# Retention followed by a GELU MLP on one core: the first w_in half triggered one step earlier, the second w_in part loaded in two halves, and a new table of the order

## The chip, the cores and the metric

The kernel runs on one core of a Trainium2 chip. The metric is the device time of one execution in microseconds, the median of 3 runs. Engines: PE is TensorE (matmuls; PEld its weight loads), DVE is VectorE, ACT is ScalarE, POOL is GpSimd, SP is SyncE. SP and ACT issue transfers on two hardware queues (q1 and q10 in the profile), POOL on a software queue (q0).

## The reference, cut to what matters

```python
# q, k, v: (4, 8, 768, 64)     w_in: (512, 2048)     w_out: (2048, 512)
state = zeros(4, 8, 64, 64); gamma = 1 - 2.0 ** (-5 - arange(8))
for t in range(768):
    state = gamma * state + outer(k[:, :, t], v[:, :, t])
    y[:, :, t] = 0.125 * q[:, :, t] @ state
x = y.transpose(0, 2, 1, 3).reshape(4 * 768, 512)
out = gelu_tanh(x @ w_in) @ w_out          # (3072, 512), float32
```

## The kernel before, in words

The recurrence is done in 6 chunks (c = 0 to 5) of 128 time steps, each for the 4 batches (b). For a chunk and a batch, q and k are scaled and cast to 16 bits (line 239; in `prep1` and `cast_in`), transposed on PE (T: line 274 in chunk 0, line 285 later) and evicted (`qkT`, line 222 on ACT, line 224 on DVE), multiplied with each other (A: line 296), masked by DVE (line 347), multiplied with v (Y: line 327) and evicted as x (line 222 on ACT). The state update is S (line 338), the part from the old state is line 315.

The MLP's first product M1 takes chunk 0 plainly (`m1_first`, matmuls in `moe1_mm`, line 428): 8 pairs of output blocks, fp = 0 to 7, each as a wide group (8 matmuls of 256 columns: batches 0 and 1) and two narrow ones (8 matmuls of 128 columns: batch 2, batch 3). The other chunks go by a scheme with 7 products instead of 8 on sums of blocks (line 551 for M1, lines 574 and 563 for M2). DVE and POOL make the sums (line 453), ACT the GELU (line 444).

w_in comes in 4 parts of 512 columns (`load_w_in`, line 409), w_out in 4 parts (`load_w_out`, line 418), all triggered by POOL and cast from 32 to 16 bits on the way. The first part of w_in is loaded in two halves (lines 601 and 602). In POOL's queue they stand behind the casts of k for batches 0 and 1 and ahead of the one for batch 2. The pair fp = 0 needs the first half alone, fp = 1 the second half (line 969: the tokens `winh` and `win`).

Before line 621 the instructions stand in the order in which the code writes them. From there on, `op` and `pe` make numbered items with needs and gives, and the table ORDER (lines 16 to 71) says in which sequence they are issued: a letter for the engine (p = PE, v = DVE, a = ACT, g = POOL, s = SP) and the item's number. "w1" is one filler matmul of line 190. The items of kind "trig" are the other 7 triggers of weights; "hold" (line 782) is a small copy on POOL that waits for the third part of w_out, and all later loads by SP (line 793) wait for it. Constants such as LANDS (line 772) and the lines 1164 and 1192 are landing times that the planner of the table assumed; they are not in the program that runs.

At the end, the last chunk's output is stored in pieces (lines 1147 to 1159): two 256 KB stores by ACT, one of 256 KB and two of 128 KB by SP. Each needs the evictions of its part.

Of the kernel before, what the change touches and what calls it, by code (L numbers as in the profile page):

```python
# [13 lines left out]


ORDER = """
p169 v9 v10 a168 a8 g0 g1 g2 g3 p181 g4 g5 g6 p179 w1 p174 a173 p172 v170 a180 p191 a190
p177 v171 g11 g7 s12 s13 p185 a178 v176 s14 s15 s16 g26 v175 s17 g29 s18 s19 s20 s21 v140
s22 g32 s23 v160 v161 g35 v163 v144 v145 v136 v141 v148 v149 p183 a182 v150 v137 v156 v157
p193 a192 p189 p187 p207 a186 p209 a208 v158 v152 v153 p223 a206 p225 p227 v138 a224 p229  # L20
v155 p195 a194 p197 a222 a228 p211 p213 a196 p231 p233 a226 a212 a210 v146 p199 p201 p215
p203 a198 a214 a202 a200 p846 v147 p217 a216 p219 p221 a218 v164 v24 a184 p847 p235 a230
a232 v25 a188 a234 p205 a204 p848 p849 v139 a220 p850 p851 p852 v165 p853 p237 v162 s36 s37
v27 v28 p240 s38 s39 s40 a238 a239 p854 p855 a856 p243 v242 v241 p246 a245 a244 p858 a859
v154 p861 g49 p249 p262 p265 p864 p865 a264 v30 v247 v248 v142 p267 v31 a236 a862 s41 p252
v166 v33 v34 a266 a250 s42 a251 s43 s44 s45 v143 s46 p866 p331 a332 p258 v151 a256 p255 p333
p316 v257 p261 v253 v254 p314 a315 v260 v259 v334 g50 v317 p867 a868 p263 p269 v268 p271
a270 p275 v274 a318 g276 g278 p297 p280 a298 a281 g55 g277 g56 s47 s48 s863 s857 g279 p299
v300 p282 v283 a335 a301 g52 g53 p273 p304 v272 a305 p287 a288 g58 g59 s61 s62 s63 s869 p338
g51 s64 p285 p302 v167 a339 a286 p292 a303 a284 g54 p309 v293 a294 s65 v310 a311 p289 p306  # L30
p378 v290 a291 v376 v377 v307 p336 a337 p343 v344 p295 a296 p319 a320 v348 p321 a322 p366
v364 p372 v365 a371 v370 a308 p323 v324 p312 a313 g352 p369 v367 p384 a382 a383 p326 v327
a328 g353 g57 a345 p340 v341 a342 v368 p329 a330 p375 v373 g60 p381 v380 v374 p870 p346 a347
g360 g361 g354 v379 p871 a325 s66 a872 p387 v385 v386 p388 p389 p391 s860 v390 p395 p393
v392 p399 v394 p401 p397 v396 g402 g404 p873 p442 s67 v400 p440 a441 p406 a407 p874 v443
v875 g349 g403 a444 p408 v409 p413 p423 p425 a414 a424 p411 v398 v426 v356 g357 v159 p457
a412 a410 p428 p418 v419 a458 a429 p430 a431 v359 g70 a78 p415 a72 a82 p459 v460 a461 p432
p447 p435 v436 g74 a76 a427 s68 s69 s86 v416 a80 a448 a437 p876 p877 p445 a446 p879 p880
g362 g405 g350 g84 s87 p464 a465 a420 p452 p462 p421 v363 g77 v79 a878 p449 a463 v83 v433
a422 g81 v355 v358 p438 a434 a417 v450 v453 p469 v470 p882 p455 p883 g476 a881 p466 a451  # L40
v351 a454 v474 v71 a439 v75 s88 a456 p885 g482 v478 g483 v467 p501 v499 p492 a500 v490 v491
g73 g85 p886 v887 a468 g475 s888 a471 p472 a473 v884 g480 s89 g95 s90 s91 s92 p893 p495 v493
g479 g486 p507 g97 v506 p504 v503 v502 v494 p889 p890 a891 s892 p894 g487 s93 p498 p509 p508
v505 p515 p511 v496 v497 p517 p521 p519 a103 a895 p513 v510 v512 a99 v514 a107 v96 p896 p897
p543 a544 v516 g522 p562 g524 p526 a527 p560 v520 v898 g105 g523 g101 g485 g102 s94 s111
a561 v518 v484 p899 p545 p900 s112 s113 g477 g525 g98 a901 p528 v529 v104 a530 p550 p548
a551 a549 s114 g110 v563 v546 a547 a564 v489 p565 p531 p902 g481 p555 p533 v556 a534 a532
v488 p567 p903 p538 a557 a109 a566 a568 v539 a540 p535 g106 v536 a537 v100 p552 v553 p905
p577 p541 a904 p906 a554 a542 a578 p584 p558 p569 p572 v108 v907 p582 v570 v573 a571 v596
a559 v594 v598 v595 s115 v599 a585 p579 v580 p908 p909 v910 s911 a583 g601 a574 s116 p575  # L50
a120 a576 g602 g603 p589 g600 g122 p586 v587 v590 p612 a581 a591 v611 p621 a588 a610 v620
p912 p913 p592 a593 v606 v607 p916 p917 a914 a619 g604 p618 s117 s118 p615 v613 v614 p624
g123 v623 a918 v617 s119 p919 p920 p922 v921 p923 g608 s915 a924 v622 p627 v616 p629 p628
p631 v625 v626 p633 v630 p639 p635 v634 v632 v638 p641 v597 p637 v636 g609 a132 g124 p925
p926 p680 p663 a664 a927 g128 g642 g644 v129 g643 p665 v666 p646 v605 a647 p648 v649 a650
v640 v133 a681 g645 p928 p929 p682 p653 v683 a654 p931 p697 a698 a126 p651 a652 p668 a669
a667 p932 v131 v933 p658 v659 g135 a684 p704 a660 p655 p670 v656 a705 v930 a671 p672 p702
v121 a703 v673 a657 p685 p661 a662 p675 p687 a688 v714 v676 v715 a674 g127 p706 s934 v707
a686 p678 a677 a679 g130 g134 g718 g719 p699 v700 p935 a701 p709 v710 a708 p689 a711 v690
a691 p936 a937 s938 p692 v693 a694 p939 p695 p712 a696 a713 v722 g716 p741 v740 v724 p732  # L60
a730 a739 p940 a941 p942 p943 v726 v727 v723 p945 p946 g725 g720 g729 v717 p747 a731 p735
v125 p738 a947 v728 v944 g721 v746 v733 v734 v736 p948 p949 a950 v745 p951 p952 v737 p748
v953 p744 p749 v742 p954 v743 p751 p753 v750 v752 p757 v756 p755 v754 g758 p955 v956 s957
g760 p796 a797 p762 a763 p779 a780 p764 v765 g759 p798 p813 v799 p815 p786 a814 v816 a800
p781 a766 v782 a787 p784 a785 p818 a819 p767 a768 p801 p788 a817 p791 v792 a783 v789 g761
p769 a770 p820 a821 p771 v772 p822 p774 p803 p777 v775 v823 a790 a793 a802 p794 a804 a795
a776 v834 g835 a773 a824 a778 p825 v826 a827 p805 v806 p808 v809 a810 g832 p962 p958 v836
p811 p828 a829 v842 a812 v830 v831 a807 v838 v843 v839 g841 a963 p959 a960 s961 p964 p966
p968 g844 g837 v840 p970 a965 p972 v845 v833 v969 v967 a971 a973 p974 a975 p976 a977 p978
v979 p980 p983 v984 v981 s982 a985 p986 p989 v987 s988 p992 a990 a991 a993 s994  # L70
"""


# [1 line left out]
def kernel(  # L75
# [25 lines left out]
    g128 = gam ** 128.0  # L101
# [480 lines left out]
    def store(eng, o, p, c, a0, a1, n0=0, n1=512):  # L582
# [14 lines left out]
    o_evT(0, AC)  # L597
    load1(AC, "k", 0, 3)
    prep1(VE, "q", 0, 1)
    prep1(PO, "k", 0, 1)  # L600
    load_w_in(0, 0, 2)
    load_w_in(0, 2, 4)
    prep1(PO, "k", 0, 2)
    spin(3)
# [28 lines left out]
        trig="g",  # L633
# [135 lines left out]
            free=[ldk],  # L769
        )  # L770

    LANDS = [0, 19.8, 22.3, 25.4, 27.5, 30.1, 32.6, 35.1]

    def trig(nm, i, n):
        load = load_w_in if nm == "win" else load_w_out
        op("trig", lambda eng: load(i), [("trig", n - 1)], [(nm, i)], early=[("trig", n)], cost=LANDS[n])

    def hold():
        T["lq", "q", 1, 0] = tile_of("lq", 0)
# [169 lines left out]
    def m1_first():  # L949
        for t0, t1, bs, cost, kind in ((0, half, (0, 1), 0.873, "gelu"), (half, half + C, (2,), 0.45, "gelu2"),  # L950
                                       (half + C, 2 * half, (3,), 0.45, "gelu2")):
            for fp in range(NP):
                key = ("bank", "h", 0, fp, t0)

                def emit(fp=fp, t0=t0, t1=t1, key=key):
                    for r in range(2):
                        moe1_mm(0, 2 * fp + r, T[key][:, r, 0:t1 - t0], t0, t1)

                def ev(eng, fp=fp, t0=t0, t1=t1, key=key):
                    g_sb[0, fp // 2] = T["g", 0, fp // 2]  # L960
                    gelu(g_tile(0, 2 * fp)[:, :, t0:t1], T[key][:, :, 0:t1 - t0])

                new = fp % 2 == 0 and t0 == 0
                al = ("al", "g", 0, fp // 2)
                op(kind, ev, [key] + ([] if new else [al]), [("H0", fp, b) for b in bs],
                   alloc=[(("g", 0, fp // 2), 1)] if new else [], early=[al] if new else [],
                   free=[key])
                last = [("m1done", 0)] if fp == NP - 1 and t1 == 2 * half else []
                pe(cost, emit, [("x", 0, b) for b in bs] + [("win" if fp else "winh", fp // 2)] + after("M1", t0),
                   [key, ("m1part", 0, fp, t0)] + last,  # L970
                   [(key, 1, (128, 2, half))], [("x", 0)])

# [188 lines left out]

    for i in range(4):
        if i < 2:
            tok["winh" if i else "win", 0] = (16.6, 15.2)[i]
    tok["m1done", -1] = 0.0
    tok["al", "x", 0] = 0.0
    T["x", 0] = xT[0]
# [16 lines left out]
    for b in (2, 3):  # L1184
        for i, nm in enumerate("qkv"):
# [3 lines left out]
            held_by[key] = [p, n, 1, 0.0]  # L1189
            slots[p][n] = None  # L1190
            T[key] = raw[nm, 0, b]
            tok[key] = ((10.0, 11.0, 11.5), (12.4, 13.3, 15.0))[b - 2][i]
    slots["bank"] = [10.8, 12.3, 11.8, 13.6] + [12.9] * 4

    tok["trig", 0] = 9.4
    for n in range(1, 8):
        trig("win" if n < 4 else "wout", n % 4, n)
    hold()
    for b in (2, 3):
        for nm in "v" if b == 2 else "qkv":  # L1200
# [93 lines left out]
```

## Time and profile before

| | |
|---|---|
| median of 3 runs | 195.65 us (195.27, 195.65, 196.06) |
| the profiled execution | 196.41 us; its span from the first to the last instruction is 194.7 us |
| granted TensorE clock | 1.000 |
| PE busy | 187.6 us, 96% |
| DVE, ACT, POOL busy | 152.0, 125.3 and 112.3 us |
| PE busy from 0 to 12 us, 12 to 19.8, 19.8 to 180 | 9.52 of 12.00, 6.24 of 7.80, 160.18 of 160.20 |
| triggers of w_in | first half 8.67 us, second half 9.6, second part 11.4 |
| landings of these | 15.37, 18.2, 20.2 us |
| last matmul group ends, last eviction ends | 191.62, 192.02 us |

The "landing" of a transfer is the time at which the instruction that waits for it may go on. Busy times of a PE group include the time in which the next group already starts; the distance between the starts of two groups is what a group costs.

### The profile page before, as it was taken

How to read it: one execution, taken by the hardware profiler on the slowest of the kernel's cores; microseconds unless marked ns; L12 is line 12 of the kernel's file. 1: busy time of each engine (PE TensorE's matmuls, PEld its weight loads, DVE VectorE, ACT ScalarE, POOL GpSimd, SP SyncE). 2: the span in 40 equal slices, each digit the busy share in tenths (PEclk: the TensorE clock that was granted, in tenths of full speed). 3: DMA queues.
4: the chain of work that ended last, by engine and by line, in shares of the span. 5: the costliest groups of instructions: out<-in, count | busy, mean ns of one | idle time of the engine just before them, and what ended most of it. 6: DMA issues, size and time to landing. Idle time of an engine off the chain costs nothing.

```text
span 194.7 us, 6611 instructions
## 1 busy us (share of the span) xinstructions
PE 187.6 (96%) x2777; PEld 152.7 (78%) x2777; DVE 152.0 (78%) x295; ACT 125.3 (64%) x244; POOL 112.3 (58%) x122
## 2 busy tenths in 40 slices
PE   7787999999999999999999999999999999999993
PEld 2455997445788788888898888888888888888882
DVE  4375029979999999989998989699878788867940
ACT  3466557065599938999357978715699820799511
POOL 2695000021389989995999984965953570814520
PEclk9999999999999999999999999999999999999999
DMA  6999999999999667998799879960020200200205
GB/s 146 288 266 204 207 206 197 220 244 216 233 224 269 145 93 141 281 203 127 142 288 258 136 123 207 259 183 0 3 108 0 111 3 3 109 0 5 108 0 215
DMA packets 96285, 30.05 MB, mean 154 GB/s; under 512 B 88320, under 2 KB 93184, under 8 KB 96256
## 3 DMA queue, kind: packets, MB, share of 16 engines
q1 hardware_dynamic: 84976, 23.35, 51.5%
q0 software_dynamic: 4752, 4.19, 13.4%
q10 hardware_dynamic: 6528, 2.10, 4.3%
q8 instruction: 21, 0.34, 0.7%
q14 instruction: 8, 0.07, 0.1%
HBM read 27.54 MB, written 6.29 MB: 174 GB/s over the span
## 4 chain that ended last, share of the span: by engine, by line
PE 89%; DMA 7%; POOL 1%; ACTq 1%; ACT 0%; issue 0%
PE ps L563 32%; PE ps L551 32%; PE ps L574 7%; PE ps L428 7%; DMA w_in<-in_moe_w_in_dram 4%; PE ps L296 3%; DMA st<-in_k_dram 3%; PE ps L327 3%; PE ps L285 2%; PE ps L315 1%; PE ps L338 1%; ACTq L162 1%; POOL qk L239 1%; POOL w_in L409 0%; ACT o L222 0%
## 5 line engine op out<-in xcount | busy, mean ns | idle before, releaser
L453 DVE TENSOR_TENSOR st<-ps,st 128x512 f32<-128x512 f32 x60 | 39.0, 679 | 5.9 <-PE ps L551 4.1
L222 ACT COPY st<-ps 128x512 f32<-128x512 f32 x60 | 32.5, 592 | 14.5 <-PE ps L551 14.3
L444 ACT ACTIVATE g<-st 128x512 f16<-128x512 f32 x60 | 36.0, 643 | 4.6 <-DVE st L453 4.5
L551 PEld LDWEIGHTS <-w_in 128*128 128x128 f16 x320 | 30.9, 98 | 4.1
L563 PEld LDWEIGHTS <-s_g 128*128 128x128 f16 x320 | 30.8, 98 | 4.0
L347 DVE TENSOR_TENSOR a<-ps,mask 128x512 f16<-128x512 f32 x44 | 27.5, 681 | 4.1 <-PE ps L296 4.0
L222 ACT COPY o<-ps 128x512 f32<-128x512 f32 (+1 forms) x28 | 14.6, 529 | 21.0 <-PE ps L563 19.8
L444 ACT ACTIVATE g<-ps 128x512 f16<-128x512 f32 (+1 forms) x44 | 21.6, 528 | 7.5 <-PE ps L428 7.0
L453 POOL TENSOR_TENSOR s_g<-g 128x512 f16<-128x512 f16 x18 | 21.3, 1184 | 8.1 <-ACT g L444 6.6
L551 PEld LDWEIGHTS <-u_w 128*128 128x128 f16 x240 | 23.2, 98 | 2.8
L563 PEld LDWEIGHTS <-g 128*128 128x128 f16 x240 | 22.9, 98 | 3.1
L551 PE MATMUL ps<-xs,w_in 128*128 128x256 f16 x160 | 22.1, 273 | 0.0
L551 PE MATMUL ps<-xs,u_w 128*128 128x256 f16 x160 | 21.6, 273 | 0.0
L551 PE MATMUL ps<-x,w_in 128*128 128x256 f16 x160 | 20.8, 273 | 0.0
L563 PE MATMUL ps<-w_out,s_g 128*128 128x256 f16 x160 | 19.8, 273 | 0.0
L563 PE MATMUL ps<-w_out,g 128*128 128x256 f16 x160 | 19.6, 273 | 0.0
L563 PE MATMUL ps<-t_w,s_g 128*128 128x256 f16 x160 | 19.3, 273 | 0.0
L453 POOL TENSOR_TENSOR xs<-x 128x512 f16<-128x512 f16 x10 | 11.7, 1174 | 11.3 <-DVE x L354 9.7
L453 POOL TENSOR_TENSOR s_g<-g,s_g 128x512 f16<-128x512 f16 x10 | 11.9, 1199 | 9.0 <-DVE s_g L453 5.7
L453 POOL TENSOR_TENSOR s_g<-s_g,g 128x512 f16<-128x512 f16 x11 | 12.8, 1166 | 6.6 <-PE ps L551 5.9
L428 PE MATMUL ps<-x,w_in 128*128 128x128 f16 (+1 forms) x192 | 15.1, 237 | 1.3 <-DMA w_in<-in_moe_w_in_dram 1.3
L239 POOL TENSOR_TENSOR v<-ld,cst 128x512 f16<-128x512 f32 x15 | 16.3, 1105 | 0.0
(74 smaller groups left out, 292.3 us busy)
## 6 DMA issues: line engine op xcount, KB each, us to landing
ld<-in_v_dram SPq DMA_DIRECT2D x19, 256.0 KB, 4.5
ld<-in_k_dram SPq DMA_DIRECT2D x17, 256.0 KB, 4.2
out_dram<-o SPq DMA_DIRECT2D x8, 512.0 KB, 3.5
ldq<-in_q_dram SPq DMA_DIRECT2D x48, 64.0 KB, 2.7
w_out<-in_moe_w_out_dram POOLq DMA_DIRECT2D x4, 512.0 KB, 16.8
w_in<-in_moe_w_in_dram POOLq DMA_DIRECT2D x3, 512.0 KB, 10.4
ld<-in_q_dram SPq DMA_DIRECT2D x5, 256.0 KB, 5.0
out_dram<-o SPq DMA_DIRECT2D x5, 256.0 KB, 4.9
```

Source lines behind the costliest of these rows:

```text
L222: eng.copy(out=out, in_=in_)
L239: eng.tensor_tensor(out=o, in0=heads(src, sw), in1=heads(cst[:, col:col + H].unsqueeze(2), sw).broadcast_to([128, NHP, 2, Dh]), op=ALU.mult,)
L285: nc.tensor.transpose(out=ps[m][j * 64:(j + 1) * 64, n + i, hp], in_=h16[nm, c, b][rows, 2 * hp + j], identity=iden[rows, rows],)
L296: nc.tensor.matmul(out=ps[j][m * 64:(m + 1) * 64, hp], lhsT=t[j * 64:(j + 1) * 64, 1, hp, m * 64:(m + 1) * 64], rhs=t[j * 64:(j + 1) * 64, ...
L327: nc.tensor.matmul(out=ps[j * 64:(j + 1) * 64, hp], lhsT=h16["v", c, b][:, 2 * hp + j], rhs=a_sb[c, b, j][:, hp], start=(c == 0), stop=Tru ...
L347: eng.tensor_tensor(out=a_sb[c, b, j], in0=ps, in1=mask[:, j], op=ALU.mult)
L428: nc.tensor.matmul(out=out, lhsT=w_in_sb[wi][:, kc, wr * 128:(wr + 1) * 128], rhs=xT[c][:, kc, t0:t1], start=(kc == 0), stop=(kc == NHP - ...
L444: nc.scalar.activation(out=out, in_=in_, func=AF.Gelu_apprx_tanh, scale=1.0)
L453: eng.tensor_tensor(out=out, in0=in0, in1=in1, op=op)
L551: nc.tensor.matmul(out=ps[:, f], lhsT=m1_lhs(lk, kc, 2 * g + f), rhs=x[:, kc], start=(n in FIRST and kc == 0 and f == 0), stop=(n in (1, 5 ...
L563: nc.tensor.matmul(out=ps, lhsT=m2_lhs(c, lk, fp, a), rhs=m2_rhs(rk, fp), start=(first and fp == 0), stop=(n in (1, 5, 6) and fp == NP - 1 ...
L574: nc.tensor.matmul(out=ps, lhsT=g_sb[0, fc // 4][:, fc % 4, b * C:(b + 1) * C], rhs=w_out_sb[fc // 4][:, fc % 4], start=(fc == 0), stop=(f ...
```

## The change: what it does

1. POOL's queue at the beginning: the trigger of w_in's first half moves from behind the cast of k of batch 1 to ahead of it. The second half's trigger stays behind that cast.
2. The second part of w_in is triggered in two halves of 256 columns; fp = 2 needs the first of them alone, fp = 3 the second. So there are 8 triggers among the items instead of 7, and all later items have a number higher by one.
3. The assumed landing times are changed with it.
4. The table ORDER is a new one as a whole. At the beginning: the transposed q and k of batches 2 and 3 are evicted by DVE (by ACT before), v of batch 3 is cast by ACT (by POOL before), PE does the transposes T of batch 3 behind the first group of M1 (ahead of it before) and A of batch 3 behind the second group of M1 (ahead of it before). At the end: the ACT store of the last chunk's first 256 KB stands behind one more eviction, and the ACT store of the second 256 KB stands behind the last eviction of all (ahead of it before); the last SP store stays.

```diff
@@ (the table: 55 lines, all of them different; its first lines)
-p169 v9 v10 a168 a8 g0 g1 g2 g3 p181 g4 g5 g6 p179 w1 p174 a173 p172 v170 a180 p191 a190
+v10 g0 p170 v169 a9 g1 g2 g3 g4 g5 v11 a12 p180 p182 p173 v172 v171 w1 p192 p175 p186 v185
...
-v979 p980 p983 v984 v981 s982 a985 p986 p989 v987 s988 p992 a990 a991 a993 s994
+v982 p987 s983 v968 p990 p993 v988 v985 a991 s989 a986 a994 a992 s995
@@
     prep1(VE, "q", 0, 1)
+    load_w_in(0, 0, 2)
     prep1(PO, "k", 0, 1)
-    load_w_in(0, 0, 2)
     load_w_in(0, 2, 4)
     prep1(PO, "k", 0, 2)
@@
-    LANDS = [0, 19.8, 22.3, 25.4, 27.5, 30.1, 32.6, 35.1]
-
-    def trig(nm, i, n):
-        load = load_w_in if nm == "win" else load_w_out
-        op("trig", lambda eng: load(i), [("trig", n - 1)], [(nm, i)], early=[("trig", n)], cost=LANDS[n])
+    LANDS = [0, 18.5, 19.9, 22.4, 25.4, 27.5, 30.1, 32.6, 35.1]
+
+    def trig(n, nm, i, *cols):
+        load = load_w_out if nm == "wout" else load_w_in
+        op("trig", lambda eng: load(i, *cols), [("trig", n - 1)], [(nm, i)], early=[("trig", n)], cost=LANDS[n])
@@
-                pe(cost, emit, [("x", 0, b) for b in bs] + [("win" if fp else "winh", fp // 2)] + after("M1", t0),
+                pe(cost, emit, [("x", 0, b) for b in bs] + [("winh" if fp in (0, 2) else "win", fp // 2)] + after("M1", t0),
@@
-    for n in range(1, 8):
-        trig("win" if n < 4 else "wout", n % 4, n)
+    trig(1, "winh", 1, 0, 2)
+    trig(2, "win", 1, 2, 4)
+    for n in range(3, 9):
+        trig(n, "win" if n < 5 else "wout", (n - 1) % 4)
```

More of the change, by code (lines that the diff above doesn't have):

```diff
@@ L16 @@
 ORDER = """
-p169 v9 v10 a168 a8 g0 g1 g2 g3 p181 g4 g5 g6 p179 w1 p174 a173 p172 v170 a180 p191 a190
[L18 to L69, printed above, removed]
-v979 p980 p983 v984 v981 s982 a985 p986 p989 v987 s988 p992 a990 a991 a993 s994
+v10 g0 p170 v169 a9 g1 g2 g3 g4 g5 v11 a12 p180 p182 p173 v172 v171 w1 p192 p175 p186 v185
@@ new lines @@
+p184 v174 v137 v138 a183 g6 g7 p194 a191 g8 a193 s13 s14 s15 a179 s16 p190 a189 s17 s18 s19
+s20 s21 s22 g30 p178 v176 v177 p208 s23 s24 p210 a209 g27 a181 p196 p212 a195 p188 v187 a207
+p214 p198 a197 p224 v140 v145 v153 p200 a199 p226 p228 p230 a225 v161 a213 a227 p216 a215
+p218 v154 p232 a217 a223 v147 v149 a229 p234 v146 p202 p236 v139 g36 g33 a201 v141 p204 a203
+v148 a211 p206 p220 p238 a237 p222 a205 v162 v164 p847 p848 p849 p850 v163 v150 v151 a235
+a219 v157 v155 a221 a233 a231 v142 v143 p851 v158 p852 p853 p854 v156 v165 v25 v26 p855 p856
@@ new lines @@
+p241 a239 s37 s38 a857 v28 v29 p247 v166 g50 s39 s40 s41 s42 v159 g51 v240 v245 v246 p859
+p244 p250 v249 v248 p263 v242 v243 v31 v32 s43 s44 s45 p862 p865 p866 a863 v34 v35 p266 a265
+s46 s47 p268 a267 p867 p253 v251 a252 p332 v152 p259 v167 p256 a860 a333 v257 v255 a258 p334
+v254 p868 a869 v335 p262 v261 v260 p315 a316 p317 v318 p264 p270 a336 a269 p274 v273 p272
+a271 g277 g279 a319 p276 g56 g57 v275 s48 s49 s864 p281 a282 g278 p283 v284 p298 a299 a53
+g54 p300 p288 g59 v301 g280 a289 p339 a340 g60 v144 s858 s870 s62 s63 s64 g52 p305 a306 s65
@@ new lines @@
+g58 g55 g61 p286 p320 p293 a287 p303 v168 v294 a302 p310 p337 a304 p379 v311 p307 v377 v378
+v308 a285 a295 a321 p290 v291 s66 a338 a312 p322 a323 p367 v365 v366 p344 v345 a292 p324 s67
+v325 p296 a297 g349 p373 v371 a372 p327 v328 p313 a346 a314 a309 g355 g350 p370 v369 v368
+p385 a383 a384 p341 v342 p871 p382 v380 p376 p330 v375 a329 a331 p347 p872 a348 a343 p388
+p390 a326 g359 a873 v381 v374 p389 p392 p396 p400 v387 v386 s68 v391 p402 p394 v393 p398
+v397 s861 g353 v395 g403 g405 p874 p424 p409 p407 a425 p426 v399 v427 a408 v410 a428 g404
@@ new lines @@
+p875 p441 p414 a415 p458 a459 p429 a430 v401 v876 p412 a413 a442 p419 p443 a79 g81 a411 g406
+p431 v357 v358 a71 v361 v362 v354 v352 v444 p433 a445 a73 v420 p416 s69 s70 p446 a447 p877
+a432 p460 p878 a879 a75 v363 p463 v417 v461 a462 v80 p448 g351 g83 g364 g74 g360 p436 p450
+p880 p881 s87 v72 a449 v437 v160 v434 a85 a421 a464 p422 p465 a435 v451 a452 a466 p883 p439
+p453 s88 a882 v356 v84 a423 p456 p467 a418 g78 g82 v454 v468 g475 a457 a77 a469 a455 a440
+p470 p884 p886 s89 v471 v477 a472 p887 v76 p473 p502 a500 g483 v885 v888 s889 s90 s91 s92
@@ new lines @@
+p493 a474 g487 v501 p890 p508 g484 v492 v491 p496 a438 g86 g479 v476 p505 g480 g96 v506 p891
+a892 v495 p894 v504 v503 s93 v507 v494 p895 s893 p499 p510 p509 p516 v497 p522 v498 p512
+g488 v511 p518 p520 v515 a100 p514 v513 v517 g523 g525 a102 a98 a896 s94 s95 a108 p897 p898
+g489 v521 p561 g110 g104 g524 a562 v478 p563 v899 v564 g526 s112 p900 p534 a535 p529 p901
+s113 a902 p527 a528 p551 a552 g103 g481 v97 g106 g485 v519 v490 s114 s115 p566 v530 p544
+p532 a567 g99 s116 a545 a531 a533 g111 p903 p556 p539 v540 a541 p570 p546 p536 v547 a565
@@ new lines @@
+p549 v537 v101 a550 v557 a548 p585 p904 p568 a569 p553 v554 a905 a586 a558 a538 p542 a543
+p906 p573 p559 v571 p576 v574 a572 p578 a579 g486 v482 v595 g596 v107 a555 p907 a577 a560
+p580 v581 v908 a575 g603 g604 p583 a584 v599 p909 p910 v911 s912 v105 s117 g598 g606 p587
+v588 a582 p590 v591 a589 g600 p913 a592 v109 p914 p593 a594 p622 p613 a611 v607 g609 v620
+g608 g602 g124 g601 v612 g610 g605 a915 s916 a621 s118 s119 p917 p918 a129 a919 p616 v615
+p619 v617 p625 v623 v624 g597 p920 v618 p921 v922 v614 p923 p924 a925 p628 p630 p629 v627
@@ new lines @@
+v626 p642 p632 v631 p634 p640 p636 v635 a133 g121 v633 p638 v637 g643 p926 g645 g125 g128
+p927 p681 v641 p647 p664 a135 g644 g646 p649 a123 a682 a648 v650 p666 a131 a665 p929 p671
+a672 p930 a928 v667 v639 s120 p683 v684 g136 a668 p669 a670 p654 p676 v677 a655 p652 a653
+p686 p932 p659 a678 v122 v130 a687 p698 a651 g127 v660 p656 v657 p673 a661 p688 p933 p705
+a685 a699 a706 v674 a689 v934 s935 p662 p679 v931 p690 a658 a663 a680 v691 v715 v716 p703
+p693 a704 a675 g719 g720 a692 p700 v701 p696 a702 a697 p710 v711 p707 v694 a695 p936 v717
@@ new lines @@
+p937 a712 v708 v723 g724 a709 p940 v134 p713 a938 a714 s939 v727 v729 p941 a942 g728 p733
+a732 p742 a731 v126 v740 v741 p943 p944 g725 v945 g721 p739 g718 g722 p736 g730 g132 v738
+p748 v734 v746 v747 p946 v737 p947 a948 p949 p950 a951 v735 p952 v726 p745 v744 v743 p750
+p749 p953 v954 p752 p754 v751 v753 p756 p758 v757 p955 p956 v755 g759 g761 v957 g760 p814
+a815 p797 p780 p763 a781 a764 p782 a798 v783 a784 p799 g762 v800 p765 v766 p768 a769 a801
+p819 p770 a820 a771 p816 v817 p772 v773 a767 a818 p785 a786 p787 a788 p775 v776 s958 p821
@@ L71 @@
+a822 a777 p802 p823 a774 p804 a805 a803 p792 v793 p778 a779 g831 g832 p789 v790 p826 v827
+a791 p809 v824 a794 a825 a828 p959 p806 v807 v810 p795 a796 p963 p812 p829 v834 v837 v835
+v833 a808 a811 v836 v838 a813 v841 a830 v843 p960 a961 v839 p965 p967 v844 a964 v840 g842
+p969 p971 s962 a966 p973 v970 v845 v846 a972 a974 p975 p977 p979 p981 a976 a978 v980 p984
+v982 p987 s983 v968 p990 p993 v988 v985 a991 s989 a986 a994 a992 s995
 """
@@ L1163 @@
         if i < 2:
-            tok["winh" if i else "win", 0] = (16.6, 15.2)[i]
+            tok["winh" if i else "win", 0] = (16.6, 13.2)[i]
     tok["m1done", -1] = 0.0
@@ L1191 @@
             T[key] = raw[nm, 0, b]
-            tok[key] = ((10.0, 11.0, 11.5), (12.4, 13.3, 15.0))[b - 2][i]
+            tok[key] = ((10.0, 11.0, 11.8), (13.0, 14.1, 15.8))[b - 2][i]
     slots["bank"] = [10.8, 12.3, 11.8, 13.6] + [12.9] * 4
     tok["trig", 0] = 9.4
-    for n in range(1, 8):
-        trig("win" if n < 4 else "wout", n % 4, n)
+    trig(1, "winh", 1, 0, 2)
+    trig(2, "win", 1, 2, 4)
+    for n in range(3, 9):
+        trig(n, "win" if n < 5 else "wout", (n - 1) % 4)
     hold()
```

## The prediction

> **What bounds the kernel now.** I read the table of engines first, then the chain that ended last, then PE's instructions in order of time where the chain leaves PE.
>
> ```profile
> span 194.7 us, 6611 instructions
> ...
> PE 187.6 (96%) x2777; PEld 152.7 (78%) x2777; DVE 152.0 (78%) x295; ACT 125.3 (64%) x244; POOL 112.3 (58%) x122
> ...
> PE 89%; DMA 7%; POOL 1%; ACTq 1%; ACT 0%; issue 0%
> ```
>
> PE is the bound: its busy time by windows is 160.18 of 160.20 us from 19.8 to 180. So a change can win only in the stretch ahead of 19.8 us or in the tail, and can lose anywhere. PE's work is the same in both programs (2777 matmuls, as many of each line). PE from 12 us on, columns start and duration:
>
> ```profile
> 12.81 0.62 PE L274 MATMUL ps<-iden,qk 128*128 128x128 f16 x8
> 13.37 0.44 PE L338 MATMUL ps<-v,qk 128*64 128x64 f16 x16
> 13.74 0.39 PE L190 MATMUL spin_ps<-zero 128*128 128x512 f16 x1
> 14.19 0.61 PE L274 MATMUL ps<-iden,qk 128*128 128x128 f16 x8
> 14.72 0.42 PE L296 MATMUL ps<-qkT 64*64 64x128 f16 x16
> 15.38 1.05 PE L428 MATMUL ps<-x,w_in 128*128 128x256 f16 x8 [0.24 <-DMA w_in<-in_moe_w_in_dram]
> 16.35 0.42 PE L296 MATMUL ps<-qkT 64*64 64x128 f16 x16
> ...
> 16.85 0.39 PE L327 MATMUL ps<-a,v 128*64 128x128 f16 x8
> 18.25 1.05 PE L428 MATMUL ps<-x,w_in 128*128 128x256 f16 x8 [1.02 <-DMA w_in<-in_moe_w_in_dram]
> ```
>
> Two waits are for w_in: 0.24 us for the first half, and 1.02 us for the second, which alone leaves PE with nothing to do. The second half's trigger ends at 9.61 and the chain gives its transfer 8.60 us: it lands at 18.21. The queues in the windows 9.6 to 12 us and 16.1 to 17.3 (packets, MB, share of the 16 engines; q0 is POOL's):
>
> ```profile
> q10 hardware_dynamic: 1535, 0.39, 71.6%
> q1 hardware_dynamic: 1212, 0.30, 56.1%
> ```
>
> ```profile
> q0 software_dynamic: 238, 0.24, 118.9%
> q8 instruction: 1, 0.02, 5.1%
> ```
>
> The first window shows no packet of q0, though the first half was handed over at 9.6. From 12 to 13 it is the same; q0 then moves 0.25 MB from 13 to 14.6 and 0.30 from 14.6 to 16.1. So both halves (0.26 MB each) were through by 16.1, and with the 0.7 us that the first half took from its last byte to its landing (14.7 to 15.37) the second was due at 16.8. It came 1.4 later. The second window shows the one other thing there: an instruction fetch of 16 KB, 5.1% of 16 engines for 1.2 us, or one DMA engine for 0.98 us.
>
> **The change, step by step.** *First half earlier.* POOL casts k of batch 0 from 5.30 to 6.34 and idles 1.34 until k of batch 1 lands and is cast at 7.68. The trigger (0.95) fits into that gap: from 6.34 to 7.29. POOL's later casts keep their times, the second half's trigger moves from 9.6 to 8.72. No transfer is added; those behind the first half (q, k, v of batch 3, issued at 5.75, 6.83 and 7.56) may each be later by what a half takes: 1.3 us (0.25 MB in 1.6 us, 0.30 in 1.5, less the start). The upper end is 1.3, the lower 0, if q0 goes on waiting for the hardware queues as above.
>
> By the Trainium skill (DMA: Bandwidth & Descriptors, "Queues, rings and completion order") each DMA engine goes round-robin between the queues that have work, a packet at a time. The fetch's place inside q0's stream agrees with that, q0's empty windows do not. What it would do here is rival (4).
>
> *What it is worth at the first M1 group.* Little: in the new order PE must have done A of batch 2 before it, and that waits for DVE, which now evicts T of batch 2 (DVE's queue: cast of q of batch 3 to 13.05, then this copy from 13.46). DVE with 128x1024 is not in the trace: its 128x512 copy of the same kind takes 0.42, ACT's 128x1024 1.01; I take 0.75, from the nearest row twice. A then runs at 14.25 to 14.67, the filler (0.39) to 15.0, M1 to 15.9; if q of batch 3 is 1.3 late, all of it 0.7 later. T of batch 3 (0.45), S (0.15) and Y (0.23) of batch 2 follow to 16.7 (17.4).
>
> *The second group* is then ready at 16.7 to 17.4, and its weights at 16.8 without the fetch, 18.2 with it: start 17.0, or 18.25 as before. Behind it come S (0.15) and A (0.35) of batch 3: done at 17.0 + 0.98 + 0.50 = 18.48. Before, the same list was done at 19.38 (S of batch 3, from 19.23). **Gain 0.9** (1.15 to 0.5); with the fetch 18.25 + 1.48 = 19.73: loss 0.35.
>
> *Second part in halves.* One more trigger on POOL (0.75 to 0.95), which has nothing behind the triggers until the copy at 32.9. The halves land at about 18.9 and 20.2 (the whole one 11.45 + 8.7 = 20.15; a half less 1.27). PE reaches fp = 2 at 18.48 + 0.9 = 19.4, fp = 3 at 20.9. It reaches the third part at 22.7, which lands then (12.2 + 10.4 = 22.6): the gain fits, with nothing to spare. POOL's ninth and tenth triggers now wait for the first and second half of part one (only the ninth did, for the first); q0's backlog of over 14 us covers that. Cost 0.
>
> *Casts and evictions moved between engines* up to 30 us: ACT and DVE idle there (DVE 0.00 busy of 4.45 from 18.25 to 22.7). Cost 0; at most the 0.1 of one late eviction.
>
> *The middle of the table* is bound by PE, and costs only where DVE comes late. I went through the queues where DVE is fullest, 42 to 54 us (11.62 of 12.00):
>
> ```profile
> 46.69 1.29 DVE L239 TENSOR_TENSOR qk<-ld,cst 128x512 f16<-128x512 f32 x2
> 47.89 1.17 DVE L453 TENSOR_TENSOR w_out<-w_out 128x512 f16<-128x512 f16 x2
> 49.22 0.43 DVE L224 COPY qkT<-ps 128x512 f16<-128x512 f16 x1 [0.17 <-PE ps L285]
> 49.56 2.47 DVE L347 TENSOR_TENSOR a<-ps,mask 128x512 f16<-128x512 f32 x4
> ```
>
> After these two casts (their k lands at about 46.9, in a chain of loads that starts at POOL's copy at 32.9 and does not move) DVE finishes the last mask product at 52.03, and PE starts its last Y at 52.53. The new order puts between them one more eviction (0.34), a sum of w_out (0.34) and an addition (0.62), and takes one sum of w_out away (0.59): 52.03 + 0.71 - 0.17 of idle time = 52.57. PE has one S more ahead of that Y (0.3): 52.83 less the 0.9 gained is 51.93. So **0.6 is given back**; with nothing gained, nothing. Elsewhere I take 0, between 0 and 0.5 lost.
>
> *The tail.* Before, the last group ends at 191.62, and:
>
> ```profile
> 189.49 0.36 ACTq L584 DMA_DIRECT2D out_dram<-o  x1
> ...
> 189.81 2.56 SPq L584 DMA_DIRECT2D out_dram<-o  x3
> 190.78 0.37 ACT L222 COPY o<-ps 128x256 f32<-128x256 f32 x1 [3.99 <-PE ps L563]
> 191.18 0.36 ACTq L584 DMA_DIRECT2D out_dram<-o  x1
> 191.65 0.37 ACT L222 COPY o<-ps 128x256 f32<-128x256 f32 x1 [0.50 <-PE ps L563]
> ```
>
> ACT stores 256 KB at 189.49 and 256 KB at 191.18; SP's last 128 KB go at 192.05, land 1.7 later, and the program ends at 194.7. After: ACT's queue is copy, store, copy, store, so its stores go at 191.18 and 192.05. In the last 2.7 us q10 moved its 0.26 MB in 25.1% of 2.7 us = 0.68 us and q1 0.14 MB in 0.41. Now both are issued together at 192.05 and share the engines: the end moves by 0.68 at most, by 0.2 at least (a 256 KB store of ACT lands in 2.1 us, SP's 128 KB in 1.9 by their medians). I take **0.65 lost**: the engines were full in those moments.
>
> Sum: -0.9 + 0.6 + 0.65 = **+0.35** on a span of 194.7. The profiled execution took 196.41 and the median is 195.65, 0.76 less; on the median's scale 195.65 + 0.35 = **196.0**.
>
> **The rivals.** (1) *The start brings nothing*: PE fetches its next instructions after about as many matmuls as before, so the fetch meets the second half again. Start +0.35, no DVE loss, tail +0.65: 195.65 + 1.0 = 196.7. It decides from a landing of 17.9 on (18.25 - 0.35). For it: the fetch's place among PE's instructions is nearly the same. Against: the half is ready up to 0.9 earlier, and 0.2 us decide whether its last packets are through. (2) *The gain stays*: DVE catches up by using its idle time before 42 us, and the two last stores overlap: -0.9 + 0.2 + a little: 194.9. (3) *The order does nothing*: the first half waits for the hardware queues as before, the second is a bit earlier, the tail's 0.2: 195.6. (4) *q0 takes turns with the hardware queues*: the halves, handed over at 7.29 and 9.6, get a third of the engines each time, are through before 14 us, and no fetch at 16.2 can hold them; the hardware loads move back by what they took, at most 2.6 us, which the waits ahead of 16.7 mostly cover. The start's 0.9 is then sure and the rest as in the sum: 196.0, the forecast's time. That turn-taking is the rule of the Trainium skill named above.
>
> **Chances.** Forecast, with (4) in it, 0.47; (1) 0.27; (2) 0.16; (3) 0.10. Range: 194.8, the low end of (2), to 197.1, (1) with 0.4 lost in the middle of the table. What a measurement can tell from no change is about 0.5%, 0.98 us: 194.67 and 196.63. Under the lower one lies a little of (2): 0.10. Over the upper one lie half of (1) and a little of the forecast with dearer ends: 0.24. Within: 0.66.
>
> **What would show it.** Right: the second M1 group starts near 17.0, PE waits for nothing up to 22.7, a DVE wait of some tenths near 52, and the last landing 2.0 us or more behind the last eviction (1.7 before). Wrong: a DMA wait of over 2 us at the second group (rival 1), no longer tail (2), or any wait on DVE or ACT over 0.5 us behind 60 us, which I have not priced.

## The result, and the profile after

The changed kernel takes 204.01 us (median of 4, 202.87 to 206.80), the kernel before 195.86 (median of 4, 195.27 to 196.11). The ratio is 1.040, 95% interval 1.0335 to 1.0468; it leaves out the run of 206.80, which counts as slow. The forecast was 196.0, within 194.8 to 197.1. The profiled execution took 203.38 us on a span of 201.7, which is 7.0 more than before's. The four runs go with PE's mean granted clock: 0.991 and 0.992 at 202.87 and 203.38 us, 0.983 at 204.65, 0.973 at 206.80. So the median lost a microsecond more than the execution that the profile shows.

The same lines of the page of the changed kernel as were shown of before (span, busy time, chain), and the granted clock in 40 slices, where the kernel before has a 9 in each:

```profile
span 201.7 us, 6614 instructions
...
PE 189.6 (94%) x2777; PEld 153.8 (76%) x2777; DVE 152.9 (76%) x298; ACT 123.5 (61%) x241; POOL 116.1 (58%) x123
...
PEclk9997999999999999999999999999999999999999
...
PE 55%; DVE 4%; issue 1%; ACT 0%; DVEq 0%
```

PE has the same 2777 matmuls and is busy 2.0 us longer; in the fourth slice its clock was not whole. DVE has come into the chain. PE's longest waits (in all, times, longest), in the changed kernel:

```profile
PE ps L296 <- DVE qkT L224: 2.7, 1, 2.7
PE ps L563 <- DVE s_g L453: 1.6, 1, 1.6
...
PE ps L551 <- DVE st L453: 0.5, 1, 0.5
```

Where the 7.0 us went is best read from equal work: I add up what each matmul takes at full clock (the distance between two starts), in PE's order, and take the time at which the sum reaches a mark. The whole sum is 175.1 us; fillers count nothing. The columns are the marks 20 to 65 and the start of the last matmul, in the profiled execution of each kernel. Times in us:

| kernel | 20 | 30 | 40 | 60 | 65 | last matmul |
|---|---|---|---|---|---|---|
| before | 33.29 | 43.38 | 54.47 | 75.46 | 80.46 | 191.34 |
| changed | 36.43 | 46.51 | 58.65 | 79.36 | 86.80 | 197.95 |
| late_trigger_new_table | 33.29 | 43.36 | 54.34 | 75.02 | 80.01 | 191.71 |
| early_trigger_old_table | 35.93 | 46.01 | 57.82 | 78.71 | 83.70 | 194.58 |
| evict_before_cast | 34.24 | 44.31 | 55.59 | 76.29 | 81.29 | 192.23 |
| fillers_in_the_gap | 34.93 | 45.00 | 56.32 | 77.03 | 82.03 | 193.72 |
| late_start_new_table | 36.37 | 46.44 | 58.59 | 79.29 | 86.89 | 198.04 |
| late_start_old_table | 35.47 | 45.55 | 57.36 | 78.25 | 83.25 | 194.13 |
| pool_braked | 36.06 | 46.13 | 58.28 | 78.98 | 83.98 | 195.68 |

The changed kernel is 3.1 us behind at 20, 4.2 at 40, 3.9 at 60, 6.3 at 65 and 6.6 at its last matmul; the tail adds 0.4. So **start 3.1, near 52 us about 1, near 85 us 2.4, tail 0.4**.

*The start.* PE in order of time:

```profile
16.60 0.42 PE L296 MATMUL ps<-qkT 64*64 64x128 f16 x16 [2.68 <-DVE qkT L224]
...
17.49 1.70 PE L428 MATMUL ps<-x,w_in 128*128 128x256 f16 x8
18.98 1.06 PE L274 MATMUL ps<-iden,qk 128*128 128x128 f16 x8
```

PE's matmul before it ended at 13.9. The A of batch 2 comes at 16.60, and behind it the first M1 group takes 1.70 us where it took 1.05, a transpose 1.06 where it took 0.61. DVE's queue says why the A is late:

```profile
15.25 0.69 DVE L239 TENSOR_TENSOR qk<-ld,cst 128x512 f16<-128x512 f32 x1 [2.69 <-DMA ld<-in_q_dram]
15.86 0.68 DVE L224 COPY qkT<-ps 128x1024 f16<-128x1024 f16 x1
```

The same cast in the kernel before, with that of k behind it:

```profile
12.36 1.44 DVE L239 TENSOR_TENSOR qk<-ld,cst 128x512 f16<-128x512 f32 x2
```

The eviction that the A needs stands behind the cast of q of batch 3, and that q landed at 15.2 instead of 12.2 (k at 16.3 instead of 13.1, v at 18.2 instead of 14.2). The queues in the window 9.6 to 12 us, where before had no packet of q0:

```profile
q0 software_dynamic: 477, 0.24, 73.6%
q10 hardware_dynamic: 1016, 0.26, 47.2%
q1 hardware_dynamic: 302, 0.07, 16.0%
```

q0 now moves 0.24 MB there, and q10 and q1 0.33 instead of 0.69. The first half landed at 13.1 (before 15.4), the second at 16.7 (18.2): neither was needed before the A.

*Near 85 us.* Six sums of g stand in a row in DVE's queue, and PE's product waits for the fifth. DVE, then POOL, in the changed kernel:

```profile
80.79 0.41 DVE L453 TENSOR_TENSOR s_g<-g 128x512 f16<-128x512 f16 x1
81.23 0.71 DVE L453 TENSOR_TENSOR s_g<-s_g,g 128x512 f16<-128x512 f16 x1
81.87 1.37 DVE L453 TENSOR_TENSOR s_g<-g 128x512 f16<-128x512 f16 x1
83.28 2.01 DVE L453 TENSOR_TENSOR s_g<-s_g,g 128x512 f16<-128x512 f16 x2
...
85.96 1.27 DVE L453 TENSOR_TENSOR st<-ps,st 128x512 f32<-128x512 f32 x2
```

```profile
80.94 0.73 POOL L224 CAST qk<-ld 128x512 f16<-128x512 f32 x1 [0.48 <-PE ps L551]
81.63 1.33 POOL L453 TENSOR_TENSOR xs<-x,xs 128x512 f16<-128x512 f16 x1
82.92 1.33 POOL L453 TENSOR_TENSOR s_g<-g 128x512 f16<-128x512 f16 x1
```

The first sum starts while POOL is idle and takes 0.41; the other five start beside POOL, which goes on up to 90 us with no gap over 0.1 us, and take 0.7 to 1.4. Each of the five ends 0.27 to 0.29 us behind the end of the POOL instruction that was running when it started: POOL's sum from 81.63 ends at 82.96, and DVE's from 81.87 ends at 83.24. So a sum of DVE's does not merely run slower, it waits for POOL's whole instruction. The two additions behind them (last line, 1.27 for both), with one operand in PSUM, take what they take elsewhere, though POOL is at work there too.

### The profile page after: what moved, and what is told of

The parts are those of the page before. It is cut to its first block, busy times and chain, and to the rows that moved or that the text cites. A ratio compares the mean times of both kernels' runs of the same rounds, so it can differ in the third digit from the quotient of the medians.

```text
span 201.7 us, 6614 instructions
## 1 busy us (share of the span) xinstructions
PE 189.6 (94%) x2777; PEld 153.8 (76%) x2777; DVE 152.9 (76%) x298; ACT 123.5 (61%) x241; POOL 116.1 (58%) x123
## 4 chain that ended last, share of the span: by engine, by line
PE 55%; DVE 4%; issue 1%; ACT 0%; DVEq 0%
PE ps L563 29%; PE ps L551 21%; DVE s_g L453 2%; PE ps L296 2%; PE ps L327 1%; PE ps L285 1%; DVE st L359 1%; DVE st L453 1%; PE ps L315 1%; PE ps L338 1%; DVE o L453 0%; DVE x L354 0%; ACT o L222 0%; DVEq L453 0%
## 5 line engine op out<-in xcount | busy, mean ns | idle before, releaser
L222 ACT COPY st<-ps 128x512 f32<-128x512 f32 x60 | 33.2, 594 | 13.7 <-PE ps L551 13.2
L444 ACT ACTIVATE g<-st 128x512 f16<-128x512 f32 x60 | 36.7, 649 | 6.4 <-DVE st L453 6.3
L453 POOL TENSOR_TENSOR s_g<-g 128x512 f16<-128x512 f16 x21 | 24.4, 1169 | 18.8 <-ACT g L444 13.6
L239 POOL TENSOR_TENSOR v<-ld,cst 128x512 f16<-128x512 f32 x15 | 15.6, 1053 | 0.8 <-DMA ld<-in_v_dram 0.7
L453 POOL TENSOR_TENSOR s_g<-s_g,g 128x512 f16<-128x512 f16 x12 | 14.6, 1214 | 2.1 <-DVE s_g L453 1.3
L428 PE MATMUL ps<-x,w_in 128*128 128x128 f16 (+1 forms) x192 | 15.6, 243 | 0.1
L453 DVE TENSOR_TENSOR o<-ps,o 128x512 f32<-128x512 f32 (+1 forms) x18 | 10.5, 595 | 6.9 <-ACT o L222 2.9
## 6 DMA issues: line engine op xcount, KB each, us to landing
w_out<-in_moe_w_out_dram POOLq DMA_DIRECT2D x4, 512.0 KB, 16.3
```

The source lines that it names most:

```text
L222: eng.copy(out=out, in_=in_)
L239: eng.tensor_tensor(out=o, in0=heads(src, sw), in1=heads(cst[:, col:col + H].unsqueeze(2), sw).broadcast_to([128, NHP, 2, Dh]), op=ALU.mult,)
L428: nc.tensor.matmul(out=out, lhsT=w_in_sb[wi][:, kc, wr * 128:(wr + 1) * 128], rhs=xT[c][:, kc, t0:t1], start=(kc == 0), stop=(kc == NHP - ...
L444: nc.scalar.activation(out=out, in_=in_, func=AF.Gelu_apprx_tanh, scale=1.0)
L453: eng.tensor_tensor(out=out, in0=in0, in1=in1, op=op)
```

## The experiments

My first theory was: three losses apart from each other, the early trigger (3.2), the new table near 52 and 85 us (3), the tail (0.4).

**1. late_trigger_new_table.** The trigger back behind the cast, table and halves as changed:

```diff
-    load_w_in(0, 0, 2)
     prep1(PO, "k", 0, 1)
+    load_w_in(0, 0, 2)
```

> The changed kernel with the first half's trigger put back behind the cast of k of batch 1; the new table and the two halves of the second part stay. Theory (three separate losses: start 3.2 us from the early trigger, about 3 us from the new table at 52 to 57 and at 85 us, 0.4 us tail): q, k, v of batch 3 land at 12.2 to 14.2 again, PE's 2.7 us wait on the eviction at 16.6 and the clock of 0.53 behind it go, the waits of 1.6 and 0.5 us near 85 us stay: 200.3 us (199.7 to 201.0). Rival A (the waits near 52 and 85 us are there only because the start is late): they go as well, 196.3 to 197.0. Rival B (the trigger is harmless, the table alone costs): the start stays as late as in the changed kernel, 203.5 to 204.5.

Measured: 196.39 us (10 runs), ratio 1.0029 (0.9992 to 1.0066). **The first theory falls**: PE's waits near 52 and 85 us went with the late start, and the time is what rival A gave. Four of DVE's same six sums in this kernel (the other two take 0.41 and 0.42), and POOL:

```profile
76.89 0.42 DVE L453 TENSOR_TENSOR s_g<-s_g,g 128x512 f16<-128x512 f16 x1
77.23 0.42 DVE L453 TENSOR_TENSOR s_g<-g 128x512 f16<-128x512 f16 x1
77.69 0.76 DVE L453 TENSOR_TENSOR s_g<-s_g,g 128x512 f16<-128x512 f16 x2
```

```profile
79.45 0.61 POOL L224 CAST qk<-ld 128x512 f16<-128x512 f32 x1 [3.33 <-DMA ld<-in_k_dram]
```

POOL stands 3.33 us for a load of k, and in that time DVE makes its sums undisturbed. In the changed kernel DVE comes to them 4.4 us later, when the load is there and POOL is at work.

A smaller loss of the same kind stays in this kernel. From the mark 65 to the last matmul it takes 111.70 us, the kernel before 110.88, and the difference arises near 98 us, where PE waits for DVE's masks. One sum ahead of these masks starts at 93.51, 0.07 us behind a sum of POOL's, and takes 1.37; in evict_before_cast (run 3) it starts 0.12 ahead of POOL's, takes 0.42, and the same stretch takes 110.94. That this one sum makes the whole difference is read from the traces and was not tested.

**2. early_trigger_old_table.** The kernel before with the trigger alone moved (the same lines the other way round).

> The kernel before with only the first half's trigger moved ahead of the cast of k of batch 1; old table, second part whole. Theory: q, k, v of batch 3 land 3 to 4 us later than in the kernel before (15.2, 16.3, 18.2), the transpose of batch 3 waits for their casts until 16.5, PE stands some 2.6 us, its clock drops to about half for 3 us; against that the 1.0 us wait at the second half goes: start +3.2, no PE wait over 0.3 us behind 25 us, 199.1 us (198.4 to 199.8). Rival A (a late start makes the waits in the middle): waits over 1 us between 50 and 90 us and 201 to 202.5. Rival B (trigger harmless): 195.0 to 196.2.

Measured: 200.14 us (197.99 to 200.75), ratio 1.018 (1.010 to 1.026). That is 0.3 above the range given. q of batch 3 is cast at 15.15, k at 16.22, and PE waits 0.99 and 0.67 us for them; then its clock is 0.50 from 18 to 20 us. Start +2.6 at the mark 20, no PE wait over 0.3 us behind 25 us; another 0.7 goes between the marks 30 and 40 (11.81 us, before 11.09). So the early trigger alone costs the start in either table, and a late start does not by itself stop PE near 85: for the waits near 85 us rival A holds in the new table only. The runs go with the clock: 0.999 in the run of 197.99, 0.983 in those of 200.6 and 200.75.

**3. evict_before_cast.** The changed kernel, one word of the table moved:

```diff
-v10 g0 p170 v169 a9 g1 g2
+g0 p170 v169 v10 a9 g1 g2
```

> The changed kernel with DVE's eviction of T of batch 2 put ahead of the cast of q of batch 3 in the table, early trigger kept. Theory (the cast, which waits for q until 15.2, holds the eviction behind it in DVE's queue): the A of batch 2 starts near 14.4 instead of 16.6, the first M1 group near 15, then PE waits 0.5 to 1 us for T of batch 3 (k cast near 16.5); the clock stays at 1.0; start 3.3 us better, waits near 85 us stay: 200.7 us (199.9 to 201.5). Rival (the late k and v of batch 3 hold PE as long at the next step): PE stands over 2 us ahead of T of batch 3 and no more than 1 us is won, 203 to 204.

Measured: 198.19 us, ratio 1.010 (1.004 to 1.016). The A starts at 14.81, PE's longest wait from 12 to 20 us is 0.55, the clock stays at 1.00, the loss at the mark 20 is 0.95 instead of 3.14, and the waits near 85 us are gone too. I had expected them to stay, by the first theory, and so the time is below the range given. The late loads hurt mostly through the one eviction queued behind a cast.

**4. fillers_in_the_gap.** The changed kernel with ten fillers in PE's gap:

```diff
-p180 p182 p173
+p180 p182 w10 p173
```

> The changed kernel with ten fillers (matmuls on zeros whose result nobody reads) put into PE's queue ahead of the A of batch 2, where PE stands 2.7 us. Nothing else is changed, so the A still starts near 16.6. Theory (the standing PE is what lets its clock drop to 0.53 in 17.5 to 20.9 us): the clock is 0.9 or more there, the same work is done 1.7 us sooner, 202.3 us (201.8 to 202.9). Rival (the clock drops for another reason, the many transfers or the casts): it drops all the same and the time stays at 203.4 to 204.5.

Measured: 200.28 us, ratio 1.020 (1.014 to 1.027). The A starts where it did; the work behind it runs at full speed:

```profile
16.62 0.42 PE L296 MATMUL ps<-qkT 64*64 64x128 f16 x16 [0.28 <-DVE qkT L224]
...
17.51 1.03 PE L428 MATMUL ps<-x,w_in 128*128 128x256 f16 x8
```

The clock in 17.5 to 20.9 us was 0.53 in the changed kernel and is 1.00 here. At the mark 20 this is 1.50 us: of the start's 3.1, **1.6 is the late A and 1.5 the clock that dropped because PE stood**. All four executions have a mean clock of 0.997 to 1.000. The time fell by more than expected, since 1.5 us earlier the six sums miss POOL's work (0.42 each).

The second theory, from here: a late PE brings DVE's work, which follows PE, beside POOL's, which follows the loads; sums with both operands in SBUF then take up to three times as long; it costs where the table puts many in a row ahead of a product.

**5. late_start_new_table and late_start_old_table.** Trigger late in both; 15 fillers behind the second M1 group, which make PE late and change nothing else in the program (first line the new table with the late trigger, second the kernel before):

```diff
-g6 g7 p194 a191
+g6 g7 p194 w15 a191
-p193 a192 p189
+p193 w15 a192 p189
```

> The kernel with the late trigger and the new table (196.39 us, no PE wait over 0.5 us behind 16 us), with 15 fillers (15 x 0.216 = 3.2 us of matmuls on zeros that nobody reads) behind PE's second M1 group. Nothing else is late: the loads, the landings and the clock stay as in that kernel, and PE is as late as in the changed kernel. New theory (in the new table DVE forms six sums of g in a row; in time with the loads they fall where POOL still waits for a load and take 0.42 us each, 3 us later they fall beside POOL's work and take 0.7 to 1.4; the same at 49 to 53 us with DVE's casts): PE waits 1 us or more on DVE's s_g near 85 us and some tenths near 52, 196.4 + 3.2 + 2 to 3 = 202.1 us (201.4 to 203.0). Rival (what stops PE near 85 us in the changed kernel comes with the early trigger itself, by other landings, and not from a late PE): 196.4 + 3.2 = 199.6 (199.0 to 200.2), no wait over 0.5 us.

> The kernel before with the same 15 fillers behind PE's second M1 group: as late, old table, which spreads those sums between POOL and DVE. New theory (it takes the new table's six sums in a row and a late PE together): 196.0 + 3.2 = 199.2 us (198.7 to 199.9), no PE wait over 0.5 us behind 25 us. Rival (any table loses when PE is late against the loads): 201 or more, with waits on DVE near 52 and 80 us. Second rival (a late PE catches up, since it waited for loads somewhere): below 198.5.

Measured: 204.15 us (202.91 to 205.38), ratio 1.044 (1.035 to 1.052), with the new table; 199.36, ratio 1.018 (1.013 to 1.023), with the old. The first repeats the changed kernel mark for mark, without its early trigger and at a clock of 0.999:

```profile
PE ps L563 <- DVE s_g L453: 1.7, 1, 1.7
...
PE ps L551 <- DVE st L453: 0.5, 1, 0.5
```

The second has no PE wait over 0.5 us behind 25 us. The first time is over 1 us above its range, the second inside. The two are not equally late: against the kernel before, the new table is 3.1 us late at the mark 20 and 4.1 at 40, the old one 2.2 and 2.9. The old table too loses 0.7 between the marks 30 and 40 (11.81 us), and its sums beside POOL near 80 to 86 us are long as well (0.62, 0.80, 0.93), but they do not stand in a row and PE does not wait for them. So the second theory holds for the loss near 85 us, and its rivals fall; near 52 us a late PE costs in both tables.

**6. pool_braked.** The changed kernel with one sum given to POOL and put ahead of the cast of k. It needs DVE's fifth sum, so POOL stands until then:

```diff
-a79 g81 a411 g406 p431 v357 v358 a71 v361 v362 v354 v352
+a79 v357 v358 v361 v362 v354 g356 g81 a411 g406 p431 a71 v352
-a882 v356 v84
+a882 v84
```

> The changed kernel, early trigger kept, with one sum of g (the fifth product's, second pair) moved from DVE to POOL and put ahead of POOL's cast of k of chunk 3, batch 2. It needs DVE's fifth sum, so that POOL stands until five of DVE's six sums are done, whatever has landed. Theory (POOL's work beside them is what makes the sums long): the five sums take about 0.42 us each, PE's waits of 1.6 and 0.5 us near 85 us shrink to 0.5 together or less, start and tail stay: 202.2 us (201.6 to 202.8). Rival (the sums are long for another reason, the transfers that run at 80 to 86 us, 230 to 280 GB/s): they stay at 0.7 to 1.4 us and the time at 203.4 or above.

Measured: 201.50 us (201.22 to 202.08), ratio 1.030 (1.024 to 1.035), 0.1 us below the range. POOL and DVE in this kernel:

```profile
82.50 1.27 POOL L453 TENSOR_TENSOR s_g<-g,s_g 128x512 f16<-128x512 f16 x1 [2.41 <-DVE s_g L453]
```

```profile
81.65 0.76 DVE L453 TENSOR_TENSOR s_g<-s_g,g 128x512 f16<-128x512 f16 x2
```

With PE almost as late as in the changed kernel (0.4 us less at the marks 20 to 60) the sums take 0.4 each, PE does not wait there, and the 2.4 us between the marks 60 and 65 are gone (5.00, as before). The transfers are as heavy as they were: 274 GB/s from 80 to 83 us, 261 in the changed kernel. POOL's work beside the sums is the cause.

**7. late_trigger_old_tail and late_trigger_new_tail.** The kernel of 1 with the last stores in the old order, beside itself:

```diff
-p984 v982 p987 s983 v968 p990 p993 v988 v985 a991 s989 a986 a994 a992 s995
+p984 v985 v982 s983 v968 a986 p987 p990 v988 s989 p993 a991 a992 a994 s995
```

> The kernel with the late trigger and the new table, its last stores put back in the order of the kernel before: ACT stores the block of the sixth product's first half ahead of the last products instead of behind the last copy but one. Theory (the new tail costs 0.4 us, two stores issued together at the end share the engines): the span ends 2.7 us behind the last copy's end, as in the kernel before, instead of 3.1, and the time is 0.4 us below that of the same kernel with the new tail (0.2 to 0.6): 196.0 us. Rival (the end is set by the last store of SP alone): no difference.

> The kernel with the late trigger and the new table once more, beside the one with the old tail: 196.4 us (196.0 to 196.8), 0.2 to 0.6 above it. Its start, middle and PE waits as in its first run.

Measured: 196.70 and 197.07 us (12 runs each), ratios 1.0044 (1.0012 to 1.0077) and 1.0048 (1.0015 to 1.0081). The times don't tell them apart. The profiles do, by 0.3: from the end of the last copy to the span's end 2.77 us with the old order, 3.05 with the new (before 2.68, changed 3.05). Most of the rest between their spans (194.1 and 195.0 us) goes with the sum near 93 us again, 0.42 with the old order and 1.38 with the new. Both medians were 0.7 above what I expected.

**8. The kernel before with parts of the change, and a version past it.** old_kernel_halves is the kernel before with w_in's second part in two transfers:

```diff
-        op("trig", lambda eng: load(i), [("trig", n - 1)], [(nm, i)], early=[("trig", n)], cost=LANDS[n])
+        op("trig", lambda eng: [load(i, *h) for h in ([(0, 2), (2, 4)] if n == 1 else [()])], [("trig", n - 1)], [(nm, i)], early=[("trig", n)], cost=LANDS[n])
```

> The kernel before with the second part of w_in as two transfers of half the columns, back to back on POOL; nothing else changed. Theory (the split costs nothing: POOL has nothing behind its triggers until 32.9 us and q0 a backlog): 195.9 us, within 0.3 of the kernel before; the halves land near 19.0 and 20.2. Rival (one more trigger of 0.75 to 0.95 us on POOL moves the later ones back, and w_out's third part, which POOL's copy at 32.9 and the loads of chunk 1 wait for): landings of the later parts 0.5 to 1 us later and 196.5 to 197.

Measured: 195.65 us (12 runs), ratio 0.999 (0.996 to 1.002): no cost. Its profile had no wait at the second M1 group at all, which left PE 0.7 us ahead up to the mark 40, and lost that in a wait of 0.90 us for a sum of x, which stood on POOL behind a cast whose load came late. So I put that sum first (g55 g277 g56 becomes g277 g55 g56), with the halves and without:

> The kernel before with the second part of w_in in halves and one more exchange in the table: POOL makes the third sum of x of chunk 1 ahead of the cast of q (chunk 2), which in the kernel with halves alone stood 1.32 us for its load with that sum behind it, and let PE wait 0.90 us at 58.79. Theory (the 0.6 to 0.7 us that the halves win at the second M1 group are kept if that wait goes): PE waits for nothing over 0.3 us behind 16 us, 195.3 us where the kernel before takes 196.0 (0.4 to 0.9 below it). Rival (PE meets the next late engine instead): a wait of about the same size elsewhere, no difference from the kernel before.

> The kernel before with only that exchange on POOL (third sum of x ahead of the cast of q of chunk 2). In the kernel before PE does not wait for this sum, so both theories expect no change: 196.0 us, within 0.3 of the kernel before. It tells what the exchange alone does in the kernel with halves.

Measured: 195.51 us (13 runs), ratio 0.9971 (0.9953 to 0.9989), and 195.46 (12 runs), ratio 0.9985 (0.996 to 1.001). The first is the only version here faster than the kernel before, by 0.3%; whether halves or sum brought it is not settled, as the intervals overlap.

These profiles also correct how I read before. Five of them share its start (before, late_start_old_table and the three of this part). PE waits 1.02 and 1.14 us for the second half in two of them, and not at all in three (second group at 17.06, 17.18 and 17.30), with an instruction fetch of 0.02 MB between 16 and 16.5 in every one. So the fetch alone does not make the wait, and what does stays open. The wait that the change was priced to remove is there in some executions only.

## Why the prediction was wrong, by its steps

- **"May each be later by what a half takes: 1.3 us ... the lower 0, if q0 goes on waiting for the hardware queues."** This is the step that failed. q0 does not wait for them: it sends nothing for 3.2 us behind the trigger's end (7.2 to 10.4; before 3.5, from 9.6 to 13.1; 2.9 to 3.6 in all fourteen traces, whether the trigger is early or late), and then has a share at once: from 10.5 to 12 it moves 0.24 MB beside 0.08 of the hardware queues, from 14 to 16 0.22 beside 0.17. I had read a delay at q0's start as a lower rank. Up to q's landing at 15.2 q0 had moved 0.42 MB, not one half's 0.25, and the loads came 3.1, 3.2 and 4.0 us late. At the 0.25 MB in 1.6 us of the kernel before, 0.42 MB are 2.7 us (an estimate), so that most of the 3.1 is q0's bytes. Rival (4) had the mechanism, but "at most 2.6 us, which the waits ahead of 16.7 mostly cover" had no row behind its second half. The rule of the Trainium skill on which it stood (DMA: Bandwidth & Descriptors, "Queues, rings and completion order": each engine goes round between the queues that have work) agrees with the trace in that nobody waits for the others to end. The third of the engines that rival (4) took for q0 it was not, from 10.5 to 12.
- **The chain to the A was right.** It had q 1.3 late move the A from 14.25 to 14.95. With the 3.1 that came, the same chain gives 16.75; measured 16.60. DVE's copy took 0.68 (0.75 taken). Only the landing was mis-sized, and what lay behind it in DVE's queue was not asked for an end of the range.
- **The clock was not in the sum.** I had counted a standing PE as its wait alone; 2.7 us of it cost 1.5 more (run 4).
- **"Elsewhere I take 0."** This step failed as well: measured 2.4 near 85 us. I took DVE's durations from a trace in which DVE and POOL met at other times. By run 5 this loss needs the late start and the new table together; run 6 ties it to the row of six sums and POOL's work beside them. The text had named a DVE wait over 0.5 us behind 60 us as what it had not priced.
- **"0.6 is given back" near 52 us:** about 1.0 in the changed kernel, nothing in run 1 with the same table (10.98 us from the mark 30 to 40; before 11.09), 0.7 in the old table when PE is late (runs 2 and 5). DVE's casts and sums there met POOL's casts in the late kernels: the four casts took 3.31 us against 2.49 in run 1. So the term was right only by sign, and that is luck: its reason, more work for DVE in the new order, cost nothing.
- **Gain 0.9 at the start:** none, and none in run 1 either (33.29 at the mark 20, as before). Rival (1), the fetch, had no part: the second half landed at 16.7, the fetch came at 17.0. The wait to be removed is not in every execution.
- **Second part in halves, cost 0:** right (0.999). **Tail 0.65:** 0.3 to 0.4: SP's last store took 2.06 us from its issue to its landing where it took 1.71 before.
- Without the early trigger the rest of the change is 196.4 to 197.1 us, near the number forecast for all of it. That is partly luck: run 1 had no gain of 0.9, no loss of 0.6, and a loss of 0.8 behind the mark 65 that the sum did not have; only the tail was in it. What it missed of the changed kernel's 7.0 us is what the trigger's own transfer sets off.

What stays open: why PE's mean clock differs between executions of one kernel, and which part of the last version's 0.3% brings it. In the three traces that show a drop it lasts 3.4 us; by this, means of 0.983 and 0.973 are two or three such stretches (an estimate), but no trace here shows those executions.

## What to carry to other kernels

When a transfer is started earlier, ask which loads share the engines with it, what is queued in order behind those loads' consumers, and put the late landing through that queue. A delay early in a kernel is more than itself: PE's clock can drop behind it, and engines that follow PE move against engines that follow the loads, so that durations from the old trace no longer hold. Where a table puts several SBUF-only operations in a row on VectorE ahead of a matmul, look at what GpSimd does in that moment.

## What the runs showed of the hardware

- DVE's sum of two SBUF operands of 128x512 f16 takes 0.40 to 0.43 us in all fourteen traces where no POOL instruction runs at its start. Where one does, with more than 0.13 us to go, the sum ends 0.27 to 0.29 us behind the end of that instruction, and so takes up to 1.40; the one exception (0.42, old_kernel_halves) started 0.02 us behind POOL's. POOL's own sum, where it starts during one of DVE's, goes from 1.16 to as much as 1.35; DVE's additions with a PSUM operand keep their 0.68. So it matters which of the two starts first, by a tenth of a microsecond. This agrees with the Trainium skill (SBUF — State Buffer, "SBUF: two separate sides"): a DVE operation with two SBUF inputs and a GpSimd operation that reads SBUF share one pair of ports, which one of them holds for its whole instruction.
- PE's granted clock fell to half behind 2.7 and 2.1 us of idle time (changed, pool_braked), and behind 0.99 and 0.67 us with 0.4 of work between (early_trigger_old_table); not behind single waits of 1.02 or 1.14 (before, old_halves_sums_first), nor behind 1.6 and 0.5 or 1.7 and 0.5 near 85 us (changed, late_start_new_table). Which idle time is enough these traces do not settle. By the Trainium skill (TensorE: Matmul & The Clock Gate, "HAM oscillation — how this bites in real kernels") gaps over about 3.4 us are what to avoid; here less was enough in three traces, and the measurement decides.
- The first transfer triggered by POOL sent its first packet 3.2 us behind the end of the trigger in the changed kernel and 3.5 in the kernel before.
